# One drain instruction more on GpSimd, between the last gather and the last five scatters of a three-stage kernel

## The chip, the cores and the metric

The kernel runs on one core of one Trainium2 chip. The metric is the device time of one execution in microseconds (us). The core has a matrix engine (TensorE, PE in the tables, its weight loads PEld), VectorE (DVE), ScalarE (ACT), GpSimd (POOL), and SyncE (SP), which here issues plain transfers. Each engine has a queue of its own, worked through in order, and engines wait for one another through semaphores.

## The reference

Three stages follow one another on 2304 tokens of width 512, in float32 (cut to what matters):

```python
# retention: 4 batches, 8 heads, 576 positions, 64 per head; no softmax
ret = scale * (q @ k.T) * Dmat                  # Dmat[i, j] = gamma_h ** (i - j) for i >= j, else 0
x = ret @ v                                     # back to 2304 x 512
# gated layer, 1536 hidden
xn = x / rms(x) * rms_g
x = (silu(xn @ w_gate) * (xn @ w_val)) @ w_out
# 8 experts, the two best of each token
noisy = x @ w_gate2 + log1p(exp(x @ w_noise)) * noise
top2, top2_w = the two largest and their softmax
for e in range(8):                              # 512 -> 1024 -> 512
    out[mask] += top2_w * (relu(x[mask] @ w1[e]) @ w2[e])
```

## The kernel before

Matrix products are done as three passes over a value split in two parts, so TensorE has most of the work. The first two stages make, 64 to 512 tokens at a time, the rows that go into the third; the rows of each token, with its two weights, are written to a table `xe` in memory, sorted by expert, by indirect transfers that GpSimd issues (`r_scat`, line 614, two for each of the 18 tiles of 128 tokens).

The third stage walks through nine segments: two for expert 0 (384 and 256 rows) and one of 640 rows (five tiles of 128) for each of experts 1 to 7. For one segment `g1` makes the hidden values (line 734 on TensorE, 736 on ScalarE, 737 on VectorE), `g2` multiplies them by the second weights into one PSUM bank per tile (line 751), and `e_out` (lines 763 and 765 on VectorE) weights the five banks and adds what was in the output before. What was there is fetched by `e_gather` (line 703, five indirect transfers) and the sum is written back by line 767 (five indirect transfers). All these indirect transfers are issued by GpSimd from its own queue. The gathers of segment g wait until the scatters of segment g-1 have landed, and the scatters of segment g wait for VectorE. Weights for the third stage are loaded by SP and split by ScalarE, VectorE and GpSimd (lines 655 to 659) well ahead.

After the last scatter the program reads the largest row count of an expert (`cmax`, line 997) on every engine and branches (line 998): if no expert has more than 640 rows, nothing is left to do but to close. On GpSimd that is: wait for the landing of its transfers, one instruction that sets the semaphores of its transfers (INC_SWDGE_SEM, line 998), and a DRAIN (line 1096, the line of the whole program). Every engine has a DRAIN there and then meets the others at a barrier, which GpSimd releases. At the start of the program stands the same: one INC_SWDGE_SEM on GpSimd, a DRAIN on each engine, a barrier (line 1088). Between the two no engine drains on the path that is run.

Of the kernel before, what the change touches and what calls it, by code (L numbers as in the profile page):

```python
# [127 lines left out]
def tile_kernel(ctx, tc, qk, vk, c64, wts, rms_g, r_gate, r_noise, noise, w1, w2, otab, cst, out):  # L128
    nc = tc.nc
# [32 lines left out]
    late = {}  # L162

    def M(shape, dt=F32):
        return psM.tile(shape, dt, tag="m", name="m")
# [478 lines left out]
    def load_w2(pr):  # L644
        e, f = divmod(pr, NFB2 // 2)
        if e >= E:
            return
        a = P['raw'].tile([128, 4, 256], F32, tag="ra", name="ra")
        nc.sync.dma_start(out=a, in_=w1[e, :, f * 256:f * 256 + 256].rearrange("(k p) f -> p k f", p=128))
        b = P['raw'].tile([128, 2, 512], F32, tag="rb", name="rb")  # L650
        nc.sync.dma_start(out=b, in_=w2[e, f * 256:f * 256 + 256, :].rearrange("(a p) d -> p a d", p=128))
        for i in range(2):
            t = wp.tile([128, 2, 4, 128], F32R, tag="w", name="w1s")
            s = a[:, :, 128 * i:128 * i + 128]
            nc.scalar.copy(t[:, 0], s)  # L655
            nc.vector.tensor_sub(t[:, 1], s, t[:, 0].bitcast(F32))  # L656
            u = wp.tile([128, 2, 512], F32R, tag="w", name="w2s")
            nc.scalar.copy(u[:, 0], b[:, i])  # L658
            nc.gpsimd.tensor_sub(u[:, 1], b[:, i], u[:, 0].bitcast(F32))  # L659
            wsp[e, 2 * f + i] = (t, u)  # L660
# [7 lines left out]
    def e_load(g):  # L668
        e, r0, n, _, _ = SEG[g]
        t = P['xr'].tile([128, n, RW], F32, tag="xr", name="xr")  # L670
        nc.sync.dma_start(out=t, in_=xe[e * NT + r0:e * NT + r0 + 128 * n, :].rearrange("(n p) d -> p n d", p=128))
        xrow[g] = t
        if g == 0:
            xT[g] = xsp[0].tile([128, 2, 4, 128 * n], F32R, tag="xs", name="xT0")
        else:
            xT[g] = P['xT'].tile([128, 2, 4, 128 * n], F32R, tag="xT", name="xT")
        if g:
            e_aux(g)
# [18 lines left out]
    def e_gather(g):  # L697
        n = SEG[g][2]
        gat[g] = P['gat'].tile([128, n, DM], F32, tag="gat", name="gat")
        if SEG[g][0] == 0:  # L700
            return
        for t in range(n):
            nc.gpsimd.indirect_dma_start(
                out=gat[g][:, t, :], out_offset=None, in_=out,
                in_offset=bass.IndirectOffsetOnAxis(ap=aux[g][1][:, t:t + 1], axis=0))

    def e_T(g, t):
        if t >= SEG[g][2]:
            return
        ps = M([128, 4, 128]) if g == 0 else P['psB'].tile([128, 4, 128], F32, tag="tp", name="tp")  # L710
        for kk in range(4):
            nc.tensor.transpose(ps[:, kk, :], xrow[g][:, t, 128 * kk:128 * kk + 128], ident)  # L712
        sl = slice(128 * t, 128 * t + 128)
        nc.scalar.copy(xT[g][:, 0, :, sl], ps)  # L714
        nc.vector.tensor_sub(xT[g][:, 1, :, sl], ps, xT[g][:, 0, :, sl].bitcast(F32))
# [5 lines left out]
    def g1(g, fb):  # L721
        e, _, n, w, _ = SEG[g]
        W = wsp[e, fb][0]
        if g == 0:
            t = hsp.tile([128, 2, 128 * n], F32R, tag="hs", name="h2")
        else:
            t = P['h2'].tile([128, 2, 128 * n], F32R, tag="h2", name="h2")
        for c0 in range(0, 128 * n, w):
            ps = psA.tile([128, w], F32, tag="gv"[gv[0] % 2], name="h")
            gv[0] += 1  # L730
            sl = slice(c0, c0 + w)
            for kk in range(4):
                for i, (a, c) in enumerate(((0, 0), (0, 1), (1, 0))):
                    nc.tensor.matmul(ps, lhsT=W[:, a, kk, :], rhs=xT[g][:, c, kk, sl],  # L734
                                     start=(kk == 0 and i == 0), stop=(kk == 3 and i == 2))
            nc.scalar.activation(t[:, 0, sl], ps, AF.Relu)  # L736
            nc.vector.scalar_tensor_tensor(t[:, 1, sl], ps, 0.0, t[:, 0, sl].bitcast(F32),  # L737
                                           op0=ALU.max, op1=ALU.subtract)
        h2[g, fb] = t

    def g2(g, *fbs):

        e, _, n, _, b0 = SEG[g]
        if 0 in fbs:
            y2[g] = [(psA if b0 + t < 4 else P['psB']).tile([128, DM], F32, tag=f"y{b0 + t}", name=f"y{b0 + t}")
                     for t in range(n)]
        hw = [(fb, h2.pop((g, fb)), wsp[e, fb][1]) for fb in fbs]
        for t in range(n):
            for fb, hh, W in hw:
                for i, (a, c) in enumerate(((0, 0), (0, 1), (1, 0))):  # L750
                    nc.tensor.matmul(y2[g][t], lhsT=hh[:, a, 128 * t:128 * t + 128], rhs=W[:, c, :],  # L751
                                     start=(fb == 0 and i == 0), stop=(fb == NFB2 - 1 and i == 2))
# [3 lines left out]
    def e_out(g):  # L756
        e, _, n, _, _ = SEG[g]
        wv, gi, si = aux.pop(g)
        y, gt = y2.pop(g), gat.pop(g)
        sc = osc.setdefault(e, [])  # L760
        for t in range(n):
            if e == 0:
                nc.vector.tensor_scalar(gt[:, t, :], y[t], wv[:, t:t + 1], None, op0=ALU.mult)
            else:
                nc.vector.scalar_tensor_tensor(gt[:, t, :], y[t], wv[:, t:t + 1], gt[:, t, :],  # L765
                                               op0=ALU.mult, op1=ALU.add)
            s = nc.gpsimd.indirect_dma_start(  # L767
                out=out, out_offset=bass.IndirectOffsetOnAxis(ap=si[:, t:t + 1], axis=0),
                in_=gt[:, t, :], in_offset=None, bounds_check=NT - 1, oob_is_err=False)
            for o in sc:  # L770
                tc.declare_no_dep(s.ins, o.ins, reason="rows differ")
            sc.append(s)
# [3 lines left out]
    with tc.manual_schedule(engines={ET.PE}):  # L776
# [74 lines left out]
        done = lambda: 36 - len(todo) - len(primed)  # L851
# [85 lines left out]
        last = NBLK - 1  # L937
# [28 lines left out]
        for fb in range(4, NFB2):  # L966
            g1(0, fb)
            g2(0, fb - 1)
            if fb >= 6:
                e_T(1, fb - 6)  # L970
        g2(0, NFB2 - 1)
        e_gather(0)
        nw = 6
        for g in range(1, NS):
            for fb in range(NFB2):
                g1(g, fb)
                if fb == 0:
                    if g > 1:
                        g2(g - 1, NFB2 - 1)
                    e_out(g - 1)  # L980
                    e_gather(g)
                elif g < NS - 1 or fb < NFB2 - 1:
                    g2(g, fb - 1)
                if fb % 2 == 1:
                    load_w2(nw)
                    nw += 1
                if g + 1 < NS:
                    if fb == 1:
                        e_load(g + 1)
                    if fb >= 3:  # L990
                        e_T(g + 1, fb - 3)
        g2(NS - 1, NFB2 - 2, NFB2 - 1)
        e_out(NS - 1)

# [105 lines left out]
```

## Time and profile before

| | |
|---|---|
| three timed runs, us | 1055.88, 1057.11 (median), 1058.38 |
| the profiled execution, us | 1056.64 |
| its span from first to last instruction, us | 1054.8 |
| TensorE busy, us | 1021.1 (97%) |
| VectorE, ScalarE, GpSimd busy, us | 445.5, 391.6, 455.9 |
| transfers read and written | 91.79 MB and 35.28 MB |

The profiled execution is 1.9 us longer than its span: what lies before the first and behind the last instruction. Busy times leave out what an engine's sequencer does by itself: waits for semaphores, branches, drains, the setting of semaphores. Such instructions have rows of their own, with a q behind the engine's name (POOLq), in the views of single lines.

### The profile page before, as it was taken

To read this page: it belongs to the slowest core of one execution; us is meant where nothing else is said; L and a number is where in the kernel's file an instruction comes from. 1 tells how busy PE (TensorE), PEld (TensorE's weight loads), DVE (VectorE), ACT (ScalarE), POOL (GpSimd) and SP (SyncE) were. 2 spreads that over 40 slices of the span, in tenths; PEclk is the share of its full clock that TensorE was granted. 3 is DMA by queue.
4 is the path that set the end of the run, shared out by engine and by line. 5 is a ranking of instruction groups with operands and counts; after the bars stand their busy time and mean duration, and the time that the engine had idled before them with its cause. 6 is when DMAs were issued, how large, how long until landed. Compare 5 with 4: busy or idle time off the path is not lost.

```text
span 1054.8 us, 15673 instructions
## 1 busy us (share of the span) xinstructions
PE 1021.1 (97%) x6190; PEld 880.1 (83%) x6190; DVE 445.5 (42%) x830; ACT 391.6 (37%) x728; POOL 455.9 (43%) x590
## 2 busy tenths in 40 slices
PE   8888999999999999999998999999999999999993
PEld 6777878888788878877997999999999999999992
DVE  3698773232522342234586253333434333342211
ACT  1235563344334533353594253333333333322110
POOL 4836875325732573246244245152433425160301
PEclk9999999999999999999999999999999999999997
DMA  8794346800300020002344156262434435250201
GB/s 302 306 398 184 96 132 235 318 1 0 145 17 1 1 81 1 1 1 81 120 134 178 61 184 215 80 191 93 157 126 169 136 113 176 65 183 1 97 1 45
DMA packets 62450, 127.12 MB, mean 121 GB/s; under 512 B 8671, under 2 KB 25439, under 8 KB 62368
## 3 DMA queue, kind: packets, MB, share of 16 engines
q1 hardware_dynamic: 53488, 97.91, 27.2%
q0 software_dynamic: 8880, 28.13, 7.5%
q8 instruction: 50, 0.82, 0.3%
q14 instruction: 32, 0.26, 0.1%
HBM read 91.79 MB, written 35.28 MB: 120 GB/s over the span
## 4 chain that ended last, share of the span: by engine, by line
PE 88%; DVE 5%; DMA 2%; issue 1%; ACT 1%; SPq 1%; POOL 1%; POOLq 0%; DVEq 0%
PE h L734 21%; PE y L751 20%; PE g L465 14%; PE v L465 14%; PE y L488 13%; DMA ck<-in_vk_dram 2%; PE tp L712 2%; PE m L517 1%; DVE m L405 1%; DVE s L278 1%; DVE m L403 1%; PE m L506 1%; DVE jo L451 1%; PE m L316 0%; PE m L312 0%
## 5 line engine op out<-in xcount | busy, mean ns | idle before, releaser
L734 PE MATMUL h<-xT,w1s 128*128 128x320 f32 (+2 forms) x1536 | 240.4, 311 | 1.1 <-ACT xT L714 0.7
L734 PEld LDWEIGHTS h<-xT,w1s 128*128 128x128 f32 x1536 | 228.1, 188 | 4.2 <-ACT xT L714 1.0
L751 PE MATMUL y<-w2s,h 128*128 128x512 f32 x960 | 231.5, 391 | 0.0
L751 PEld LDWEIGHTS y<-w2s,h 128*128 128x128 f32 x960 | 177.2, 188 | 33.6
L659 POOL TENSOR_TENSOR w2s<-rb,w2s 128x512 fp32r<-128x512 f32 x64 | 83.2, 1302 | 202.8 <-ACT w2s L658 202.6
L488 PE MATMUL y<-jo,hs 128*128 128x512 f32 x648 | 162.0, 396 | 2.4 <-DVE jo L451 1.3
L465 PE MATMUL v<-xs,jv 128*128 128x512 f32 (+1 forms) x720 | 163.5, 375 | 0.0
L465 PE MATMUL g<-xs,gs 128*128 128x512 f32 (+1 forms) x720 | 161.7, 373 | 0.0
L488 PEld LDWEIGHTS y<-jo,hs 128*128 128x128 f32 x648 | 120.6, 188 | 31.8 <-DVE jo L451 1.6
L465 PEld LDWEIGHTS v<-xs,jv 128*128 128x128 f32 x720 | 124.4, 188 | 26.3 <-issue 1.3
L465 PEld LDWEIGHTS g<-xs,gs 128*128 128x128 f32 x720 | 125.1, 188 | 24.3 <-issue 0.4
L737 DVE SCALAR_TENSOR_TENSOR h<-h,h 128x320 fp32r<-128x320 f32 (+2 forms) x128 | 62.5, 490 | 144.6 <-ACT h L736 136.1
L451 POOL TENSOR_TENSOR jo<-orr,jo 128x512 fp32r<-128x512 f32 x48 | 63.3, 1318 | 126.4 <-ACT jo L450 120.3
L736 ACT ACTIVATE h<-h 128x320 fp32r<-128x320 f32 (+2 forms) x128 | 55.8, 436 | 153.8 <-PE h L734 140.9
L656 DVE TENSOR_TENSOR w1s<-ra,w1s 128x512 fp32r<-128x512 f32 x64 | 57.6, 899 | 122.0 <-ACT w1s L655 112.7
L475 DVE TENSOR_TENSOR sg<-sg,v 128x512 f32<-128x512 f32 (+1 forms) x60 | 37.9, 632 | 167.8 <-PE v L465 167.0
L655 ACT CAST w1s<-ra 128x512 fp32r<-128x512 f32 x64 | 39.6, 619 | 114.9 <-PE y L751 64.0
L443 POOL TENSOR_TENSOR jv<-vr,jv 128x512 fp32r<-128x512 f32 x48 | 62.4, 1300 | 38.5 <-ACT jv L442 38.4
L767 POOL DMA_INDIRECT out_dram<-gat,si x40 | 40.1, 1004 | 80.9 <-DVE gat L765 64.5
L450 ACT CAST jo<-orr 128x512 fp32r<-128x512 f32 x60 | 37.2, 621 | 81.4 <-PE v L465 79.3
L471 ACT ACTIVATE sg<-g 128x512 f32<-128x512 f32 (+1 forms) x60 | 33.2, 554 | 82.5 <-PE g L465 74.5
L442 ACT CAST jv<-vr 128x512 fp32r<-128x512 f32 x60 | 37.1, 620 | 53.6 <-PE y L488 49.1
(140 smaller groups left out, 982.7 us busy)
## 6 DMA issues: line engine op xcount, KB each, us to landing
raw<-in_wts_dram SPq DMA_DIRECT2D x36, 512.0 KB
ra<-in_moe_w_dram SPq DMA_DIRECT2D x32, 512.0 KB
rb<-in_moe_w_dram SPq DMA_DIRECT2D x32, 512.0 KB
xr<-xe SPq DMA_DIRECT2D x7, 1290.0 KB
xe<-z SPq DMA_DIRECT2D x8, 1032.0 KB
ck<-in_qk_dram SPq DMA_DIRECT2D x16, 512.0 KB
ck<-in_vk_dram SPq DMA_DIRECT2D x16, 512.0 KB
out_dram<-z SPq DMA_DIRECT2D x6, 768.0 KB
```

Source lines behind the costliest of these rows:

```text
L443: (nc.gpsimd if it // NFB < NBLK - 1 else nc.vector).tensor_sub(t[:, 1], s, t[:, 0].bitcast(F32))
L451: (nc.gpsimd if it // NFB < NBLK - 1 else nc.vector).tensor_sub(t[:, 1], s, t[:, 0].bitcast(F32))
L465: nc.tensor.matmul(ps, lhsT=W[:, a, kk, :], rhs=X[:, c, :], start=(kk == 0 and i == 0), stop=(kk == 3 and i == 2))
L488: nc.tensor.matmul(yps[blk][t], lhsT=hh[:, a, 128 * t:128 * t + 128], rhs=W[:, c, :], start=(fb == 0 and i == 0), stop=(fb == NFB - 1 and ...
L655: nc.scalar.copy(t[:, 0], s)
L656: nc.vector.tensor_sub(t[:, 1], s, t[:, 0].bitcast(F32))
L659: nc.gpsimd.tensor_sub(u[:, 1], b[:, i], u[:, 0].bitcast(F32))
L734: nc.tensor.matmul(ps, lhsT=W[:, a, kk, :], rhs=xT[g][:, c, kk, sl], start=(kk == 0 and i == 0), stop=(kk == 3 and i == 2))
L736: nc.scalar.activation(t[:, 0, sl], ps, AF.Relu)
L737: nc.vector.scalar_tensor_tensor(t[:, 1, sl], ps, 0.0, t[:, 0, sl].bitcast(F32), op0=ALU.max, op1=ALU.subtract)
L751: nc.tensor.matmul(y2[g][t], lhsT=hh[:, a, 128 * t:128 * t + 128], rhs=W[:, c, :], start=(fb == 0 and i == 0), stop=(fb == NFB2 - 1 and i ...
L767: s = nc.gpsimd.indirect_dma_start(out=out, out_offset=bass.IndirectOffsetOnAxis(ap=si[:, t:t + 1], axis=0), in_=gt[:, t, :], in_offset=No ...
```

## The change

One instruction is added: a DRAIN on GpSimd. It has no semaphore to wait for and sets none. A dependence without a semaphore puts it behind the last transfer that `e_gather` issued, and it stands in the program ahead of the last products and of the `e_out` of the last segment.

```diff
         if SEG[g][0] == 0:
             return
         for t in range(n):
-            nc.gpsimd.indirect_dma_start(
+            late['gathered'] = nc.gpsimd.indirect_dma_start(
                 out=gat[g][:, t, :], out_offset=None, in_=out,
                 in_offset=bass.IndirectOffsetOnAxis(ap=aux[g][1][:, t:t + 1], axis=0))
...
                     if fb >= 3:
                         e_T(g + 1, fb - 3)
+
+        done = nc.gpsimd.drain()
+        tc.add_manual_dep(done.ins, late['gathered'].ins.name, mybir.DependencyInfo(
+            mybir.DependencyClass.NoSync, mybir.DependencyReason.DATA), reason="behind the last gather")
         g2(NS - 1, NFB2 - 2, NFB2 - 1)
         e_out(NS - 1)
```

These are the last rows of GpSimd's queue before the change, from the gathers of the last segment but one on (`gat` is the tile that a gather fills, `si` and `gi` the row numbers, `w2s` the split second weights):

```order
L703 DMA gat<-out_dram,gi 128x512 x5
L659 TENSOR_TENSOR w2s<-rb,w2s 128x512
L690 CAST si<-xr 128x5
L659 TENSOR_TENSOR w2s<-rb,w2s 128x512 x3
L767 DMA out_dram<-gat,si 2304x512 x5
L703 DMA gat<-out_dram,gi 128x512 x5
L767 DMA out_dram<-gat,si 2304x512 x5
L997 TENSOR_LOAD cmax
L998 COMPARE_AND_BRANCH
```

This list names no drains. In the changed program the same rows stand in the same order, and the new DRAIN is between the last L703 row and the last L767 row; nothing moved on any engine, and later lines have numbers higher by four.

## Rows read from the trace of the kernel before

**Rows 1.** The page: span, busy time by engine, and the chain that ended last.
```profile
span 1054.8 us, 15673 instructions
PE 1021.1 (97%) x6190; PEld 880.1 (83%) x6190; DVE 445.5 (42%) x830; ACT 391.6 (37%) x728; POOL 455.9 (43%) x590
PE 88%; DVE 5%; DMA 2%; issue 1%; ACT 1%; SPq 1%; POOL 1%; POOLq 0%; DVEq 0%
```
**Rows 2.** Busy time by stretch: length, engines (instructions), granted clock, transfers' share, GB/s.
```profile
1000.00:1033.00 33.00, 33.00 (x188) 30.15 (x187) 5.67 (x11) 4.37 (x10) 0.00 (x0) 1.00 0.03 12
1040.00:1044.00 4.00, 0.00 (x0) 0.00 (x0) 0.00 (x0) 0.00 (x0) 0.00 (x0) 0.50 0.08 27
1044.00:1055.00 11.00, 0.00 (x0) 0.00 (x0) 0.00 (x0) 0.00 (x0) 0.00 (x0) 0.50 0.00 0
```
**Rows 3.** The chain that ended last, its final pieces: start us, us, what.
```profile
1030.74 1.40 PE y L751 x6
...
1032.23 0.76 DVE gat L765
...
1039.01 0.92 POOL out_dram L767
```
**Rows 4.** Line 998, GpSimd alone: count, ns min/median/max, first and last start.
```profile
L998 POOLq EVENT_SEMAPHORE  x6: 17/30/43, 1041.8 to 1042.2; - x6
L998 POOLq INC_SWDGE_SEM  x1: 2408/2408/2408, 1042.3 to 1042.3; - x1
```
**Rows 5.** Line 1096, the close: GpSimd and SP from 1044 to 1054, then whole.
```profile
L1096 POOLq DRAIN  x1: 9147/9147/9147, 1044.8 to 1044.8; - x1
L1096 POOLq EVENT_SEMAPHORE  x1: 17/17/17, 1054.0 to 1054.0; - x1
...
L1096 SPq EVENT_SEMAPHORE  x12: 28/28/28, 1044.7 to 1045.4; - x12
L1096 SPq DRAIN  x2: 7/7/7, 1045.4 to 1045.5; - x2
...
L1096 POOLq DRAIN  x3: 40/107/9147, 1044.8 to 1054.5; - x3
L1096 ACTq DRAIN  x2: 8/8/8, 1034.1 to 1054.2; - x2
L1096 PEldq DRAIN  x2: 8/8/8, 1037.9 to 1054.3; - x2
L1096 DVEq DRAIN  x2: 10/14/17, 1042.3 to 1054.2; - x2
```
**Rows 6.** What SP's queue waited for: us in total, times, longest.
```profile
SPq L1096 <- DMA out_dram<-gat,si: 112.2, 1, 112.2
SPq L1096 <- PEq L1096: 9.2, 2, 8.6
```
**Rows 7.** Line 1088, the opening, on GpSimd.
```profile
L1088 POOLq INC_SWDGE_SEM  x1: 27/27/27, 0.1 to 0.1; - x1
L1088 POOLq DRAIN  x1: 172/172/172, 0.3 to 0.3; - x1
```
**Rows 8.** The three lines of GpSimd that issue transfers, over the whole span.
```profile
L614 POOL DMA_INDIRECT xe<-R,si x36: 956/964/1418, 270.4 to 595.2; - x36
...
L703 POOL DMA_INDIRECT gat<-out_dram,gi x35: 942/948/1587, 645.8 to 998.7; - x35
...
L767 POOL DMA_INDIRECT out_dram<-gat,si x40: 972/982/1119, 611.4 to 1039.0; - x40
```
**Rows 9.** GpSimd in order of time: start us, us; idle before it and its releaser.
```profile
270.43 1.21 POOL L614 DMA_INDIRECT xe<-R,si  x1 [1.00 <-DVE si L600]
...
998.69 0.95 POOL L703 DMA_INDIRECT gat<-out_dram,gi  x1 [0.30 <-issue]
1033.80 1.00 POOL L767 DMA_INDIRECT out_dram<-gat,si  x1 [34.16 <-DVE gat L765]
```
**Rows 10.** Line 767 on GpSimd between 999 and 1034 us: its waits.
```profile
L767 POOLq EVENT_SEMAPHORE  x3: 43/5501/30412, 997.0 to 1002.6; - x3
```
**Rows 11.** TensorE and VectorE from 999 to 1012 us, in order of time.
```profile
1006.25 3.68 PE L734 MATMUL h<-xT,w1s 128*128 128x320 f32 x24
...
1001.73 0.49 DVE L737 SCALAR_TENSOR_TENSOR h<-h,h 128x320 fp32r<-128x320 f32 x1 [4.69 <-ACT h L736]
1003.49 0.49 DVE L737 SCALAR_TENSOR_TENSOR h<-h,h 128x320 fp32r<-128x320 f32 x1 [1.27 <-ACT h L736]
```

## The prediction

> **What bounds the kernel now.** The page comes first: TensorE is busy for 97% of the span and holds 88% of the chain that ended last [rows 1], so nearly every stage is bound by TensorE, and an edit on GpSimd counts only where TensorE has run out of work. The table of stretches shows where that is: from 1040 us to the end of the span, at 1054.8, no engine has one instruction, and from 1044 on the transfers' share is 0.00 [rows 2]. The chain of waits agrees and stops there: its final pieces are products that end at 1032.1, VectorE's sums, and the last scatter, whose issue ends at 1039.9 [rows 3]. These views leave out what a sequencer does by itself, so the last 15 us have to be read from the rows of single lines. There GpSimd waits until 1042.2 for the landing of its scatters, spends 2.408 us in INC_SWDGE_SEM from 1042.3, then 9.147 us in a DRAIN from 1044.8, and goes to the barrier at 1054.0 [rows 4, 5]. SP has come to the same barrier at 1045.5 and is held there for 8.6 us [rows 5, 6] (that row names PE's sequencer as releaser, but TensorE came to the barrier at 1037.9, and GpSimd last). The end of the program is thus bound by two sequencer instructions of GpSimd, 11.56 us together.
>
> **What the long drain does.** It doesn't wait for data: GpSimd's waits for landing are over at 1042.2, 2.5 us before it starts, and nothing is moved while it runs [rows 2, 4]. A drain as such isn't dear: GpSimd's two others at the close take 0.107 and 0.040 us, the one at the opening 0.172 [rows 5, 7], and no transfer of GpSimd lies between them and the drain (or the start) before. Behind the long one lie all of the program's indirect transfers: 36 + 35 + 40 = 111 [rows 8]. I read it as a pass over what GpSimd keeps of each transfer since the last drain: 9.147 / 111 = 0.0824 us for each. That the two that follow are short says that nothing is left to go through then. The trace has one such drain only, so whether the price goes by the count or is a lump that any transfer brings about isn't seen; that is the main uncertainty.
>
> The Trainium skill has a rule that speaks against the change: VectorE: DVE Perf Modes, "The DRAIN you can't avoid", says that the drains at a program's beginning and end take a constant of about 12 ns on all engines. The rows agree for SP (7), ScalarE (8) and VectorE (10 to 17 ns) and disagree for GpSimd (9147) [rows 5]; taken alone the rule would leave nothing to save, and the time where it is.
>
> **The change, part by part.**
>
> The added drain stands behind 106 of the 111 transfers. By the count it takes 106 x 0.0824 = 8.73 us; its bounds are 0.04 us and 9.15 us. It starts at 999.6, when the last gather's issue ends (998.69 + 0.95) [rows 9], or, if it waits for the gathers to land, at 1002.6, when GpSimd's wait for VectorE starts, the last of its three [rows 10]. So it ends by 1011.8 at the latest. What hides it is that wait: 30.4 us, until 1033.0, for VectorE's first sum [rows 10]. Behind the drain in GpSimd's queue stand only those waits and the five scatters, and GpSimd runs nothing else between 1000 and 1033 [rows 2]; no other engine waits for GpSimd there, since VectorE sees the gathers land by their own semaphores. 21 us of cover are left: cost 0. Without cover it would be the whole 8.73.
>
> The drain at the close has five transfers left: 5 x 0.0824 = 0.41 us, 8.73 less (0.82 if the five gathers weren't done when the first drain passed). Not all of that reaches the end, for SP is late next: its twelve waits and its drain run from 1044.7 to 1045.5, and its hold at the barrier, 8.6 us, can shrink only to what the release takes from GpSimd's drain on, about 0.2 (1053.9 to 1054.1, the end of 8.6 us from 1045.5). The end moves by **8.4 us**.
>
> INC_SWDGE_SEM takes 2.408 us here and 0.027 at the opening [rows 4, 7]. The two don't do the same, but both kinds of instruction are short where no transfer lies behind them and long at the close. Bounds: nothing saved, or 2.4. I take it by the count, as for the drain: 0.03 + 2.38 x 5 / 111 = 0.14, saving **2.3 us**. This passes through to the end, since SP's twelve waits start when this instruction is over: SP's wait for the scatters' semaphores, 112.2 us long, ends where it ends [rows 5, 6]. VectorE is the next after that, at 1042.3 [rows 5], about a microsecond before SP's new 1043.2, and costs nothing.
>
> The first scatter behind a drain might be slower: the first of the program took 1.21 us and the usual one 0.96 [rows 8, 9]. Bounds 0 and 0.25; I take 0, since the scatter that follows 34 us of idleness took 1.00 already [rows 9].
>
> Sum against the profiled execution: 1056.64 - 8.4 - 2.3 = 1045.9 us. The median of the runs is 0.5 above that execution, so the forecast for the median is **1046.4 us**, 1.0% less. About 0.2% (2.1 us) can be told from no change.
>
> **The rivals.**
>
> - Only the drain goes by the count; INC_SWDGE_SEM stays at 2.4 us because setting eight semaphores is its work. For it: the opening one may have had none to set. Against it: 2.4 us is long for any sequencer instruction here, where one wait takes 17 to 43 ns. 1057.1 - 8.4 = 1048.7 us.
> - The price is a lump that any transfer since the last drain brings about. For it: only one such drain is seen, and a fixed round over queues would look the same. Against it: it would be the only fixed cost of that size on a sequencer. Then the added drain takes 9.1 us under cover and the last one 9.1 us again: 1057.1 us, no change. The constant that the Trainium skill gives (VectorE: DVE Perf Modes, cited above) would come to the same time by another size of the lump.
> - The change doesn't do what it says: the gathers are still in flight at 999.6, and a drain that passes over nothing unless all transfers are done would leave the work to the end. For it: five gathers land as late as 1002.6. Against it: then the last drain, with everything landed, would be the only kind that works. 1057.1 us.
> - The drain's work holds VectorE up while it runs beside products, which the drain at the close couldn't show, as no engine worked beside it. Were VectorE held from 999.6 to 1008.8, its pieces of 1001.7 and 1003.5 would come at 1008.8 instead, and TensorE's next products, which start at 1006.25 and take the banks that these pieces free [rows 11], would lose up to 9.15 - (1006.25 - 1001.73) = 4.6 us: 1051.0 us.
> - Slower: the drain holds GpSimd's queue beyond its cover, because beside running work it is far slower than alone. It begins to cost at 1033.0 - 999.6 = 33.4 us, 3.7 times the price at the close, and is a loss on balance once it takes over 33.4 + 10.7 = 44.1 us; at 50 us the time would be 1046.4 + 16.6 = 1063.0. Nothing in the trace suggests such a factor.
>
> **How the numbers follow.** Both instructions by the count 0.60, the drain alone 0.20, the lump 0.10, no effect for the gathers in flight 0.03, VectorE held 0.04, slower 0.03. The predicted time is the first's, 1046.4. The first two, with the runs' own scatter of about 1.3 us around their median, lie between 1045.0 and 1050.0, which holds 0.8. Faster by over 0.2%: 0.60 + 0.20 + 0.04, less a little for a drain that shrinks but partly, 0.84; same 0.13; slower 0.03.
>
> **What the profile would show.** The changed line should have a DRAIN of GpSimd of 8 to 9 us that begins near 1000 us, with the first scatter still at 1033.8 after VectorE; the long DRAIN of the close should be 0.4 to 0.8 us, INC_SWDGE_SEM 0.1 to 0.3 us, SP's longest hold at the last barrier 0.2 us, and the span 1044.1. A close that still drains for 9 us would show the lump and a time within 0.2%; an INC_SWDGE_SEM of 2.4 us the second case. A prediction wrong in sign would show the first scatter later than 1033.8, with GpSimd released by its own drain.

## The result, and the profile after

The changed kernel takes 1046.13 us (median of five runs, 1044.75 to 1049.46) against 1057.11 before: 0.9901 of the time, 95% interval 0.9888 to 0.9914. Forecast were 1046.4 us and a range from 1045.0 to 1050.0.

The page of the changed kernel has the same work and a span 10.6 us shorter than in [rows 1] (1054.756 and 1044.149 us in the traces, which the pages round); the one instruction more is the drain:

```profile
span 1044.1 us, 15674 instructions
PE 1020.7 (98%) x6190; PEld 880.0 (84%) x6190; DVE 446.2 (43%) x830; ACT 391.9 (38%) x728; POOL 454.9 (44%) x590
```

The line of the added drain (count, ns min/median/max, first and last start):

```profile
L993 POOLq DRAIN  x1: 13045/13045/13045, 995.6 to 995.6; - x1
```

GpSimd in order of time, the last gather and the first scatter, which answer to [rows 9]:

```profile
998.94 0.95 POOL L703 DMA_INDIRECT gat<-out_dram,gi  x1 [0.30 <-issue]
1033.96 1.00 POOL L767 DMA_INDIRECT out_dram<-gat,si  x1 [34.08 <-DVE gat L765]
```

GpSimd's waits at line 767 between 999 and 1034 us, which answer to [rows 10]:

```profile
L767 POOLq EVENT_SEMAPHORE  x3: 43/43/24269, 1008.7 to 1008.9; - x3
```

The drain is recorded from 995.6 to 1008.6, 13.0 us. It begins in the record while three of the five gathers ahead of it are still to be issued, so what it takes itself is read from the end of the last gather's issue, 999.89 (998.94 + 0.95): 8.74 us. The wait for VectorE, 30.4 us before, starts at 1008.9 and still lasts 24.3 us; the first scatter is released by VectorE as before, 0.16 us later.

The close, in the rows of line 1002 (998 before) and 1100 (1096 before), which answer to [rows 4] and [rows 5]:

```profile
L1002 POOLq EVENT_SEMAPHORE  x6: 17/30/43, 1041.7 to 1042.2; - x6
...
L1002 POOLq INC_SWDGE_SEM  x1: 288/288/288, 1042.3 to 1042.3; - x1
```

```profile
L1100 SPq EVENT_SEMAPHORE  x14: 17/28/28, 1042.5 to 1044.1; - x14
...
L1100 POOLq DRAIN  x3: 46/107/474, 1042.6 to 1043.9; - x3
L1100 SPq DRAIN  x3: 7/7/7, 1043.3 to 1043.6; - x3
...
L1100 DVEq DRAIN  x2: 10/14/17, 1042.4 to 1043.6; - x2
```

What SP waited for, as in [rows 6]:

```profile
SPq L1100 <- DMA out_dram<-gat,si: 110.5, 1, 110.5
SPq L1100 <- PEq L1100: 0.7, 2, 0.5
```

INC_SWDGE_SEM starts when it did, at 1042.3, and takes 0.288 us in place of 2.408; the long drain takes 0.474 in place of 9.147. GpSimd is done with it at 1043.1, and SP, whose row of twelve waits now starts at 1042.5, reaches the barrier at 1043.3: SP is the last. Its two holds at barriers together fell from 9.2 to 0.7 us.

VectorE beside the drain, in order of time, which answers to [rows 11]:

```profile
1001.89 0.49 DVE L737 SCALAR_TENSOR_TENSOR h<-h,h 128x320 fp32r<-128x320 f32 x1 [4.69 <-ACT h L736]
1003.65 0.49 DVE L737 SCALAR_TENSOR_TENSOR h<-h,h 128x320 fp32r<-128x320 f32 x1 [1.27 <-ACT h L736]
```

Same durations, same idle times before them (4.69 and 1.27 us): the drain doesn't hold VectorE.

### The profile page after: what moved, and what is told of

Read it like the earlier page. It is cut to its first block, busy times and chain, and to the rows that moved or that the text cites. A ratio compares the mean times of both kernels' runs of the same rounds, so it can differ in the third digit from the quotient of the medians.

```text
span 1044.1 us, 15674 instructions
## 1 busy us (share of the span) xinstructions
PE 1020.7 (98%) x6190; PEld 880.0 (84%) x6190; DVE 446.2 (43%) x830; ACT 391.9 (38%) x728; POOL 454.9 (44%) x590
## 4 chain that ended last, share of the span: by engine, by line
PE 89%; DMA 4%; DVE 2%; ACT 1%; POOL 1%; SPq 1%; issue 1%; POOLq 0%; DVEq 0%; ACTq 0%
PE h L734 22%; PE y L751 21%; PE g L465 14%; PE v L465 14%; PE y L488 14%; DMA ck<-in_vk_dram 3%; DMA raw<-in_wts_dram 2%; PE tp L712 2%; PE m L517 1%; PE m L506 1%; DVE jo L451 1%; PE m L312 0%; PE m L371 0%; SPq L174 0%; PE m L316 0%
## 5 line engine op out<-in xcount | busy, mean ns | idle before, releaser
L465 PEld LDWEIGHTS g<-xs,gs 128*128 128x128 f32 x720 | 125.1, 188 | 24.3 <-issue 0.4
L767 POOL DMA_INDIRECT out_dram<-gat,si x40 | 40.4, 1010 | 81.1 <-DVE gat L765 65.1
```

The lines of the kernel that those rows point to most:

```text
L465: nc.tensor.matmul(ps, lhsT=W[:, a, kk, :], rhs=X[:, c, :], start=(kk == 0 and i == 0), stop=(kk == 3 and i == 2))
L767: s = nc.gpsimd.indirect_dma_start(out=out, out_offset=bass.IndirectOffsetOnAxis(ap=si[:, t:t + 1], axis=0), in_=gt[:, t, :], in_offset=No ...
```

## The experiments

The changed kernel shows that the drain moves under cover, but not yet why the one at the close is short. After it, a drain that goes by the count of transfers and one that is dear only the first time look alike: the first took 8.7 us and the second 0.5. Four kernels tell more. In what follows "left" is the number of GpSimd's transfers since its last drain, and ratios are to the kernel before as it ran beside these four (1057.43 us, median of 19 runs).

**The drain early.** It is moved behind the gathers of expert 1, with 46 transfers ahead of it and 65 behind:

```diff
                     e_out(g - 1)
                     e_gather(g)
+                    if g == 2:
+                        done = nc.gpsimd.drain()
...
-        done = nc.gpsimd.drain()
...
```

> The one added drain is moved ahead: behind the gather of expert 1, so that 46 transfers lie before it and 65 behind it. By the count (0.0824 us a transfer): the added drain takes about 3.8 us of its own, the drain at the close 5.4 us, INC_SWDGE_SEM about 0.19 + 65 x 0.02 = 1.5 us, and the time is 1046.1 + 1.2 + (5.4 - 0.75) = 1052 us. If the first drain behind any transfer pays a single price and later ones are cheap (the changed kernel cannot tell this apart): the added drain takes about 9 us, the close about 0.5 us, and the time is that of the changed kernel, 1046 us.

Measured: 1052.48 us, 0.9953 of the kernel before (0.9938 to 0.9967). Its rows, the drain moved ahead, then line 1003, then the close:

```profile
L983 POOLq DRAIN  x1: 9585/9585/9585, 647.4 to 647.4; - x1
```

```profile
L1003 POOLq INC_SWDGE_SEM  x1: 1488/1488/1488, 1042.6 to 1042.6; - x1
```

```profile
L1101 POOLq DRAIN  x3: 46/107/5374, 1044.2 to 1050.1; - x3
```

GpSimd in order of time behind that drain:

```profile
650.95 0.95 POOL L703 DMA_INDIRECT gat<-out_dram,gi  x1 [0.30 <-issue]
657.17 1.29 POOL L659 TENSOR_TENSOR w2s<-rb,w2s 128x512 fp32r<-128x512 f32 x1 [5.27 <-ACT h L736]
```

A drain had been made before the close, and the close still takes 5.374 us, with 65 transfers left: the first-time price is refuted, and the count gave 5.4 and 1.5. The moved drain ends at 657.0 (647.4 + 9.585), 5.1 us after the last gather's issue, where the count gives 46 x 0.0824 = 3.8. The other 1.3 us are looked at further down.

**The drain late.** It is moved behind the last scatter, without cover:

```diff
-        done = nc.gpsimd.drain()
...
         e_out(NS - 1)
+        done = nc.gpsimd.drain()
+        tc.add_manual_dep(done.ins, osc[E - 1][-1].ins.name, ...)
```

> The added drain stands behind the last scatter, where nothing covers it. By the count: it takes 9.1 us and what the last scatter still needs to land, the drain at the close then 0.1 us, and INC_SWDGE_SEM is down to about 0.2 us although no work was saved. The load of the row count and the branch come behind the drain, so the time is about 1057 to 1059.5 us: no gain, or a loss of up to 2.5 us. If INC_SWDGE_SEM does not go by the transfers left since the last drain, it stays at 2.4 us, and the time is 1059 to 1062.

Measured: 1056.33 us, 0.9992 of before (0.9981 to 1.0004). The drain, line 1002 with GpSimd's branch, the close, and the last scatter in order of time:

```profile
L995 POOLq DRAIN  x1: 10683/10683/10683, 1038.3 to 1038.3; - x1
```

```profile
L1002 POOLq EVENT_SEMAPHORE  x6: 17/30/43, 1052.2 to 1052.7; - x6
L1002 POOLq COMPARE_BRANCH  x1: 57/57/57, 1049.7 to 1049.7; - x1
L1002 POOLq INC_SWDGE_SEM  x1: 183/183/183, 1052.7 to 1052.7; - x1
```

```profile
L1100 POOLq DRAIN  x3: 34/53/107, 1053.0 to 1054.2; - x3
```

```profile
1038.91 0.97 POOL L767 DMA_INDIRECT out_dram<-gat,si  x1 [0.30 <-issue]
```

The drain ends at 1049.0, 9.15 us after the last issue's end at 1039.9: all 111 transfers, at 0.0824 each, and nothing on top for the landing of the last ones, whose last bytes move at 1041.2, while the drain runs. With none left, INC_SWDGE_SEM takes 0.183 us and the drain of the close, the first of the three in its row, 0.053. So both prices follow the transfers left, and nothing is won by it: the price is paid ahead, in the same place on the path. The time is 0.7 us below the low end of what was expected. The landing of the last scatters, which the expectation added, takes nothing on top here; whether that is all of the 0.7 wasn't tried.

These rows also bear on the prediction's reading of the close. The branch ends at 1049.7 and GpSimd's waits behind it come only at 1052.2, 2.5 us later, though the scatters' last packet (a piece of a transfer) ended 8.5 us before the branch. The kernel before has a like stretch, from its branch at 1039.0 to the waits at 1041.8 [rows 4]:

```profile
L998 POOLq COMPARE_BRANCH  x1: 53/53/53, 1039.0 to 1039.0; - x1
```

The prediction and the text ahead of it read this stretch as the wait for the scatters to land. The late drain has it with nothing left to land, so the landing isn't what sets it there; what fills it isn't shown. The added drain doesn't touch it: it is 2.6 us in the changed kernel.

**A drain behind every group of gathers.** Seven, one for each of experts 1 to 7:

```diff
                     e_gather(g)
+                    if g > 1:
+                        done = nc.gpsimd.drain()
...
-        done = nc.gpsimd.drain()
...
```

> A drain behind the gathers of each of experts 1 to 7: seven in place of one. By the count: the first takes about 3.8 us and the others 0.8 to 1.0 us, each with the wait for its gathers to land; the close is as in the changed kernel, 0.47 us and 0.29 us, and the time 1046 us, as GpSimd's subtractions behind each drain have idle time ahead of them. If a drain has a price of its own of several us, the six extra ones show it, and the subtractions that TensorE needs may come late: 1047 to 1055 us. If only the first drain is dear, the first takes 9 us.

Measured: 1046.16 us, 0.9906 of before (0.9879 to 0.9933), not to be told from one drain. The seven drains, the close, the last gather and GpSimd's waits behind the seventh drain:

```profile
L983 POOLq DRAIN  x7: 7392/7898/9209, 645.7 to 994.3; - x7
```

```profile
L1101 POOLq DRAIN  x3: 46/107/464, 1041.2 to 1042.4; - x3
```

```profile
997.64 0.95 POOL L703 DMA_INDIRECT gat<-out_dram,gi  x1 [0.30 <-issue]
```

```profile
L767 POOLq EVENT_SEMAPHORE  x3: 43/43/28639, 1002.4 to 1002.6; - x3
```

The seventh drain has ten transfers left, 0.82 us by the count, but it ends at 1002.3 (994.3 + 8.07), 3.7 us after the last gather's issue (998.6). What lies between is the landing. In the view of transfers, one packet moves on GpSimd's queue, q0, between 1001.5 and 1001.6, and from 1001.6 to 1002.4 none on any queue:

```profile
q0 software_dynamic: 1, 0.00, 0.6%
```

```profile
DMA packets 0, 0.00 MB, mean 0 GB/s; under 512 B 0, under 2 KB 0, under 8 KB 0
```

The six drains with ten left, those of experts 2 to 7, end 3.0 to 3.8 us after their last issue, but all of them 0.76 to 0.85 us after the last packet of q0: the price of ten by the count, from the landing on. So a drain also waits until the transfers ahead of it have landed, which the prediction had left open. The Trainium skill has it in a general form (PSUM — Partial Sum Buffer, "Engine vs sequencer instructions": a drain waits for the engine to go fully idle); these drains agree, if transfers in flight count as not idle. It costs nothing here: the time with seven drains is that with one.

**Ten small transfers more.** The kernel before, without a drain, with ten transfers of 16 elements of 4 bytes. They were meant for the last wait, but the scheduler put them at 169 us; for the count this makes no difference.

```diff
+        few = P['aux'].tile([128, 10], F32, tag="few", name="few", bufs=1)
+        for i in range(10):
+            nc.gpsimd.dma_start(out=few[0:16, i:i + 1], in_=cst[0:16, i:i + 1])
         g2(NS - 1, NFB2 - 2, NFB2 - 1)
```

> The kernel before, with ten transfers of GpSimd more, each of 16 elements of 4 bytes, under the cover of the last wait for VectorE; no drain is added. By the count of transfers: 121 of them, so the drain at the close takes 121 x 0.0824 = 9.97 us and INC_SWDGE_SEM 2.6 us. If the price goes by bytes or by rows, ten such transfers add nothing that shows: 9.15 us and 2.41 us.

Measured: one run of 1055.37 us, within the 1054.13 to 1059.71 us of the kernel before, which says nothing of the time; the rows of the profile are what counts. The small transfers, line 1001, and the close:

```profile
L994 POOL DMA_DIRECT2D few<-in_cst_dram x10: 484/487/772, 169.0 to 176.3; - x10
```

```profile
L1001 POOLq INC_SWDGE_SEM  x1: 2620/2620/2620, 1040.1 to 1040.1; - x1
```

```profile
L1099 POOLq DRAIN  x3: 46/99/9958, 1042.8 to 1053.3; - x3
```

Ten transfers of 64 bytes add 0.811 us to the drain (9.958 - 9.147), 0.081 each; the 111 of the kernel before, 75 of them of 256 KB, cost 0.082 each. Bytes and rows don't count, transfers do. Nor is it the time since the last drain, which is about the same in the two kernels. The measured closes side by side:

| transfers left | kernel | DRAIN at the close, us | INC_SWDGE_SEM, us |
|---|---|---|---|
| 0 | drain late | 0.053 | 0.183 |
| 5 | the changed kernel | 0.474 | 0.288 |
| 5 | seven drains | 0.464 | 0.288 |
| 65 | drain early | 5.374 | 1.488 |
| 111 | the kernel before | 9.147 | 2.408 |
| 121 | ten small transfers | 9.958 | 2.620 |

A line through the second and the last row, (9.958 - 0.474) / 116 = 0.0818 us a transfer from 0.065 us on, gives 5.38 and 9.14 for 65 and 111 transfers; for the semaphores (2.620 - 0.288) / 116 = 0.0201 us a transfer from 0.188 on, which gives 1.49 and 2.42. (INC_SWDGE_SEM stands just ahead of the drain of the close, so both are counted from the same earlier drain.)

## Why the prediction was right, step by step

- **The long drain is a pass over the transfers since the last drain, 0.0824 us each.** The price by the count is shown, at five counts from 0 to 121 and whatever the size of a transfer: 0.0818 us each and 0.065 us beside. That it is a pass over records that GpSimd keeps is a reading that fits; no row shows the records. The constant that the Trainium skill gives for such drains (VectorE: DVE Perf Modes, "The DRAIN you can't avoid") holds for GpSimd in none of these rows: where no transfer is left it comes nearest, at 0.03 to 0.17 us (the opening's 0.172 among them).
- **The added drain costs 8.73 us and is covered by GpSimd's wait for VectorE.** 8.74 us, ended at 1008.6 with 24 us of cover to spare. That the cover is what saves the time is shown by the late drain: the same price in the open, and a ratio of 0.9992. With ten left a drain's price starts at the landing (the kernel with seven). With 106 left none of that wait shows: the last packet ends at 1002.5, long before the drain does, and the price runs from the last issue on, so the later of the two starts that the prediction allowed for didn't apply.
- **The drain at the close falls to 0.41 us, and SP is the next to be late; 8.4 us.** 0.474 us; SP does reach the barrier last, 0.2 us behind GpSimd, and its hold there fell from 8.6 to 0.2 us, which is 8.4 (of the two holds in its row, 9.2 before and 0.7 after, the second barrier has 0.6 and 0.5).
- **INC_SWDGE_SEM goes by the count as well; 2.3 us.** By the count it does, but from 0.18 us on and not from 0.03: the opening's 0.027 us was no measure of what is fixed in it. It fell to 0.288 where 0.14 was forecast, and saved 2.1. The prediction's second case, in which it stays at 2.4, falls with this.
- **The sum.** 10.7 us forecast; the spans differ by 10.6 us, 8.4 and 2.1 by the two terms, and the medians by 11.0. That the median came within 0.3 us of the forecast is partly chance: single runs of the changed kernel lie up to 4.7 us apart.

Of the rivals, the lump that any transfer brings about falls with the 0.474 us of the close, which has five transfers left, and a price paid by the first drain alone with the 5.374 us of the early drain; the drain that does nothing while gathers are in flight falls with the close of 0.474; VectorE held falls with its unchanged rows (its price of 4.6 us was too high besides: held until 1008.8, the piece of 1001.73 comes 7.1 us late, 2.6 beyond the slack of 4.5 that the prediction reckons); a drain slower beside running work falls with 8.74 us beside TensorE's products. What the prediction said of the record was off in two places. The drain's row starts at 995.6 and not near 1000, while gathers ahead of it are still to be issued, and so its 13.0 us are not its price. And what it read as GpSimd's wait for the landing of its scatters, up to 1042.2, is a stretch behind the branch that the kernel with the late drain has as well, with nothing left to land. Neither is a term of the sum.

Left open is the early drain's 1.3 us beyond the count. The last packet of its gathers ends at 654.6 and the drain at 657.0, 2.4 us later; the first of the seven drains, also with 46 left, ends 2.2 us after its own. With the whole 3.8 us behind the landing the early drain would have ended at 658.4, and with no wait for it at 655.7. So a part was done ahead of the landing and a part had to wait for it; which transfers wait, no row shows.

## What to carry to other kernels

Where GpSimd issues transfers, read the rows of the sequencer at the program's close and count the transfers since GpSimd's last drain: here each costs 0.10 us there (0.082 in the drain, 0.020 in the setting of semaphores) after all engines are done. A drain put into a long wait of GpSimd pays for them where nobody waits; one is enough if few transfers follow it, and it has to stand where the transfers ahead of it may land without holding up work behind it. The views of busy time don't show any of this: the sign is a tail of the span in which no engine is busy and no data moves. Of that tail some 2.5 us behind GpSimd's branch are still there, and no run here tried to shorten them.

## What the runs showed of the hardware that wasn't expected

INC_SWDGE_SEM has a fixed part of 0.18 us, which its opening row of 0.027 us didn't show, beside the 0.020 us for each transfer. A transfer of 64 bytes costs as much at the close as one of 256 KB. A drain of GpSimd with ten transfers left ended 0.76 to 0.85 us after the last packet of those transfers, whenever that was. The row of a drain may start before the transfers ahead of it are issued, so that 13.0 us are recorded for 8.74 us of its own.
